# Three small edits where attention hands over to the experts: earlier weight requests, a shorter step list for one group, three subtractions on GpSimd

## The chip, the core and the metric

The kernel runs on one core of a Trainium2 chip. The metric is the device time of one execution in microseconds (us), the median over several runs. TensorE (PE) multiplies, with weight loads shown as an engine of their own (PEld); VectorE (DVE), ScalarE (ACT) and GpSimd (POOL) do the elementwise work; SyncE (SP) issues most of the DMAs, and GpSimd those that gather or scatter by index.

## The reference, cut to what matters

```python
a = softmax(phi)                                  # phi: 8 batches, 8 heads, 576 rows, 32 memories
k_m, v_m = a^T k, a^T v                           # 32 memory rows for each head
x = softmax(q k_m^T / 8) v_m                      # attention; rows become 4608 tokens of 512
e = argmax(x @ w_gate)                            # one of 8 experts for each token
gate = softmax(x @ w_gate)[e] * sigmoid(x @ w_output_gate)[e]
out[token] = gate * (relu(x @ w1[e]) @ w2[e])     # w1: 512x1024, w2: 1024x512
```

## The kernel before, in words

**Attention** is walked in 20 groups `g` (four pairs of batches, five groups each). A loop over `t` gives each group its steps in the order of a list of letters, `ORDER`, or an entry of `ORDERS` for some `t`: `S` scores turned and their maximum taken (`S0` is the transpose alone, `S1` the rest), `X` the exponential on ACT, `D` the division (a DVE sum, a POOL product), `B` a transpose back, `V0` the value product on PE and its copy `xo` on ACT, `V1` the store of `xo` to the DRAM table `xs`, `C` the scores of the next group, `M` and `m` memory work, `R` routing work. `LAG` says by how many `t` a step trails. `X1` and `D1` are the steps of one group earlier.

**The experts** work on slots of three (later two, one) blocks of 128 tokens. At group 17's `S0` the loop stops, and the first slot begins (`run`). From here attention goes on inside the slots: `hook` is called after each piece of PE work (in a three-block slot: 8 times in the first product, 12 times in the second) and takes three steps of the attention list and two of the routing. So an entry of the list decides at which piece of the expert's PE stream an attention step is put. A first-product piece is 12 matmuls `bps<-xh,whl` and `bps<-xl,whl` of 128x384, a second-product piece 6 matmuls `bps<-whl,hh` and `bps<-whl,hl` of 128x512.

**Weights** come in pieces `w` of 128x1024 (512 KB), eight for each slot, by SP's queue (`fetch`, L588). `split` makes two parts of a piece: ACT casts it to fp32r (`whl`, high, L599), and `flush` has DVE subtract that from `w` (`whl`, low, L613). PE multiplies in three passes: high by high, high by low, low by high. `parted` counts the pieces made; at the subtraction of the first slot's fourth, sixth and eighth piece it stands at 4, 6 and 8. Five buffers hold `w`, four hold `whl`.

**Routing.** When the last group of a batch pair has left, `rank` finds each token's expert and its place (`lm`, `w__2076`, `pm`, `ohg`, then a PE product `pr` with `strict`, L996, then `w__2076` again at L1006), writes the gates `gt` to columns of `xs` by four small DMAs on SP (L1025, L1028), and builds one-hot tables `Aw` on POOL (L1035). The gate stores of the second pair are held back until `run` begins. `route_early` and `table` then give the lists of token indices (`counts` is the PE product at L288, `bwb` feeds the one at L245). POOL gathers a slot's tokens `xg` by such a list (L550), the first slot's gates once more (`gidx`, L558), and scatters finished rows `y` (L1283). `y` has two buffers, so ACT's third `y` of a slot waits for the first scatter. The PSUM banks `ps` are three until the second slot has ended; `bpd` has two, shared by values, scores and the transposes `bpd<-ident,xg` (L1136) that turn the next slot's tokens.

```python
hh = relu(bank)              # ACT, L1314
hl = max(bank, 0) - hh       # DVE, L1315: after it the bank is free
```

Of the kernel before, what the change touches and what calls it, by code (L numbers as in the profile page):

```python
# [8 lines left out]
F32 = mybir.dt.float32  # L9
# [4 lines left out]
ALU = mybir.AluOpType  # L14
# [4 lines left out]
B, H, S, D, M = 8, 8, 576, 64, 32  # L19
# [19 lines left out]
ORDERS = {14: ["R0", "X", "S", "m", "V0", "M", "V1", "R1", "M", "m", "R2", "D", "B", "C"],  # L39
# [3 lines left out]
STEPS14 = {"R0": 12, "R1": 1, "R2": 8}  # L43
LAG = {"X": 1, "B": 2, "D": 1, "V": 3, "C": -1}
TICK = 0
# [30 lines left out]
def attention_moe(tc, phiT, kv, qT, wgo, wall, out):  # L76
    nc = tc.nc
    V, A, G, T = nc.vector, nc.scalar, nc.gpsimd, nc.tensor

    with contextlib.ExitStack() as ctx:  # L80
# [406 lines left out]
        def force():  # L487
            clock[0] += 1
            (rou if rou.gens else late if late.gens else att).step()
# [37 lines left out]
        m = NPE + NPT  # L527
# [27 lines left out]
        def gather_gates(z):  # L555
            V.tensor_scalar(gidx[:], z["idx"][0][:, 0:3], 2, None, ALU.logical_shift_left)
            for k in range(z["nb"]):
                G.indirect_dma_start(  # L558
                    out=z["xg"][:, k, 0:XQ], out_offset=None,
                    in_=xs[0:z["rows"]].rearrange("t (a q) -> (t a) q", a=4),  # L560
                    in_offset=bass.IndirectOffsetOnAxis(ap=gidx[:, k:k + 1], axis=0),
                    bounds_check=4 * z["rows"] - 1, oob_is_err=False)
# [5 lines left out]
        class Stream:  # L568
# [40 lines left out]
            def flush(self):  # L609

                if self.half:
                    w, hl = self.half
                    V.tensor_tensor(hl[:, 1], w[:], hl[:, 0].bitcast(F32), ALU.subtract)  # L613
                    self.half = None

            def take(self, i, u):
# [17 lines left out]
        def gathers(i, must=0):  # L634

            while gat[0] < min(gat[1], i + xgs.size):
                z = order[gat[0]]
                if not z["listed"]:
                    if gat[0] >= must:
                        break  # L640
                    force()
                    continue
                gather(z)
                gat[0] += 1
# [496 lines left out]
        def turn_first(z):  # L1141

            xg, n = z["xg"], z["nb"] * P
            xh, xl = z["x"] = mo.tile([P, 4, 3 * P], F32R, name="xh"), mo.tile([P, 4, 3 * P], F32R, name="xl")
            p0, p1, p2 = bank([512], "ps"), banks(), banks()
            pts = [p[:, 0:n] for p in (p0, p1[:, 0], p1[:, 1], p2[:, 0])]
            for c, pt in enumerate(pts):
                for k in range(z["nb"]):
                    T.transpose(pt[:, k * P:(k + 1) * P], xg[:, k, c * XQ:c * XQ + P], ident[:])
            for c, pt in enumerate(pts):  # L1150
                A.copy(xh[:, c, 0:n], pt)
                V.tensor_tensor(xl[:, c, 0:n], pt, xh[:, c, 0:n].bitcast(F32), ALU.subtract)  # L1152
# [255 lines left out]
        def settle():  # L1408

            att.finish()  # L1410
            pso.close()
            pa.close()
            env["hs"] = ctx.enter_context(tc.tile_pool(name="hs", bufs=1, side="right", reuse_waits="tile"))
            env["rl"] = ctx.enter_context(tc.tile_pool(name="rl", bufs=1, side="right", reuse_waits="tile"))
            env["xt"] = ctx.enter_context(tc.tile_pool(name="xt", bufs=2, side="right", reuse_waits="tile"))

            env["rep"] = env["rl"].tile([P, 4, P], BF16, name="rep")
            i4 = ident[:].rearrange("p (b i) -> p b i", b=4)
            for b in range(4):
                V.tensor_copy(env["rep"][:, b].rearrange("p (a i) -> p a i", a=4),  # L1420
                              i4[:, b:b + 1].to_broadcast([P, 4, 32]))
            grow(1)
            env["ps"] = ctx.enter_context(tc.tile_pool(name="p1", bufs=7, space=PSUM, reuse_waits="tile"))

        def run(st):

            lo, hi = st.lo, st.hi // 8
            while not order[lo]["known"]:
                force()
            while held:  # L1430
                held.pop(0)()
            st.fetch()
            if lo:
                gat[:] = lo, hi

            hooks = itertools.count()

            def hook():
                n = next(hooks)
                if lo == 0 and n == GATES[1]:  # L1440
                    gather_gates(order[0])
                if lo or n >= GATES[0]:
                    gathers(i)
                clock[0] += not att.gens
                att.step(HOOK[0])
                (rou if rou.gens else late).step(HOOK[1])

            for i in range(lo, hi):
                if i or lo:
                    gathers(i, i + 1)  # L1450
                if i == 0:
                    turn_first(order[0])
                    st.split(2)
                elif i == lo:
                    for c in range(5):
                        turn_x(order[i], c)

                def nxt(c):
                    if i + 1 < hi:
                        gathers(i, i + 2)  # L1460
                        turn_x(order[i + 1], c)

                if order[i]["nb"] > 1:
                    several(i, st, nxt, hook)
                else:
                    single(i, st, nxt)
                if "hs" not in env and (i == LAST or not att.gens):
                    settle()
# [5 lines left out]
        env["open"] = True  # L1474
        n = NPE + NPT + NPP
        run(stream)
        used = nc.values_load(slot[0:1, NSLOT:], min_val=0, max_val=NSS)  # L1477
        with tc.If(used > 0):
            run(Stream(n, n + 1))
            with tc.If(used > 1):  # L1480
                run(Stream(n + 1, n + 4))
                with tc.If(used > 4):
                    run(Stream(n + 4, NSLOT))
# [44 lines left out]
```

## Time and profile before

| what | value |
|---|---|
| median of 3 runs | 547.72 us (547.4 to 549.03) |
| the profiled execution's own time | 548.07 us |
| its span, first to last instruction | 546.3 us |
| PE busy | 507.7 us, 93% |
| DVE, ACT, POOL busy | 354.3, 286.6, 232.2 us |
| first expert matmul | 110.2 us |

The profiled execution lies 0.35 us above the median, and its span 1.77 us below its own time. The table is read thus: where PE is busy all the time, a change counts only if it takes away time in which PE waits, or adds some.

### The profile page before, as it was taken

Reading aid. Unit: us, or ns where it says so; the run is one execution under the profiler, and the core shown is the slowest. Engines: PE = TensorE matmul, PEld = TensorE weight load, DVE = VectorE, ACT = ScalarE, POOL = GpSimd, SP = SyncE. Lnnn points to the kernel's source line nnn. Section 1 sums busy time; section 2 is a strip of 40 time slices with the busy share of each in tenths; the row PEclk is TensorE's granted clock in tenths of the full one; section 3 lists DMA queues with packets and bytes.
Section 4 is the critical chain, followed back from the end, with each engine's and each line's share of the span. In section 5 each row is a group of like instructions: output and inputs, shape, how many; then the busy total and the mean of one; then the engine's idle time right before and its main releaser. Section 6 shows DMA issues by size and latency. Waiting matters only on the chain. (4 is left out here: it accounts for less than half of the span.)

```text
span 546.3 us, 10599 instructions
## 1 busy us (share of the span) xinstructions
PE 507.7 (93%) x3866; PEld 437.1 (80%) x3868; DVE 354.3 (65%) x798; ACT 286.6 (52%) x536; POOL 232.2 (43%) x239
## 2 busy tenths in 40 slices
PE   3788877999999999999999999999999999999993
PEld 2555555687789898897998989898999899898982
DVE  4275999869775569979446456953876297639310
ACT  3466775563444465353434546853776376548210
POOL 2242644616744052610278374565437453721101
PEclk9968998999999999999999999999999999999998
DMA  7999999997557758754465585865786577743001
GB/s 290 416 389 383 411 391 394 362 332 230 151 179 243 265 194 294 217 154 131 148 201 172 149 279 148 258 219 189 213 252 194 168 249 231 238 139 94 30 20 43
DMA packets 42093, 123.75 MB, mean 227 GB/s; under 512 B 10304, under 2 KB 10368, under 8 KB 41648
## 3 DMA queue, kind: packets, MB, share of 16 engines
q1 hardware_dynamic: 35136, 102.71, 56.7%
q0 software_dynamic: 6896, 20.28, 10.8%
q8 instruction: 32, 0.52, 0.4%
q14 instruction: 29, 0.24, 0.1%
HBM read 102.62 MB, written 20.35 MB: 225 GB/s over the span
## 5 line engine op out<-in xcount | busy, mean ns | idle before, releaser
L1347 PE MATMUL bps<-whl,hh 128*128 128x512 f32 x640 | 192.2, 393 | 0.0
L1310 PE MATMUL bps<-xh,whl 128*128 128x384 f32 x640 | 166.2, 336 | 0.7 <-DVE hl L1315 0.7
L613 DVE TENSOR_TENSOR whl<-w,whl 128x1024 fp32r<-128x1024 f32 x112 | 136.3, 1221 | 14.8 <-ACT whl L599 14.8
L1347 PEld LDWEIGHTS bps<-whl,hh 128*128 128x128 f32 x640 | 119.9, 188 | 24.4
L599 ACT CAST whl<-w 128x1024 fp32r<-128x1024 f32 x112 | 116.9, 1048 | 16.6 <-PE bps L1347 13.6
L1310 PEld LDWEIGHTS bps<-xh,whl 128*128 128x128 f32 x640 | 115.8, 188 | 2.3 <-DVE hl L1315 1.0
L544 POOL DMA_INDIRECT xg<-xs,idx_ql x84 | 100.4, 1195 | 25.7 <-issue 22.9
L1310 PE MATMUL bps<-xl,whl 128*128 128x384 f32 x320 | 107.1, 335 | 0.2 <-DVE xl L1152 0.2
L1347 PE MATMUL bps<-whl,hl 128*128 128x512 f32 x240 | 93.7, 390 | 0.0
L1315 DVE SCALAR_TENSOR_TENSOR hl<-bps,hh 128x384 fp32r<-128x384 f32 x80 | 43.7, 554 | 60.3 <-ACT hh L1314 60.3
L1314 ACT ACTIVATE hh<-bps 128x384 fp32r<-128x384 f32 x80 | 38.4, 494 | 64.6 <-PE bps L1310 64.5
L1283 POOL DMA_INDIRECT out<-y,idx_ol x23 | 25.4, 1106 | 102.9 <-ACT y L1282 54.3
L1310 PEld LDWEIGHTS bps<-xl,whl 128*128 128x128 f32 x320 | 60.1, 188 | 0.7 <-DVE xl L1152 0.4
L1347 PEld LDWEIGHTS bps<-whl,hl 128*128 128x128 f32 x240 | 45.1, 188 | 8.6
L903 POOL TENSOR_TENSOR ea<-ea,mx 128x512 f32<-128x512 f32 (+1 forms) x20 | 20.1, 1007 | 49.9 <-DVE mx L901 48.1
L1305 PE MATMUL bps<-xh,whl 128*128 128x384 f32 x128 | 37.7, 338 | 0.0
L1306 PE MATMUL bps<-xh,whl 128*128 128x256 f32 x128 | 35.7, 279 | 0.0
L1282 ACT ACTIVATE y<-bps,gx 128x512 f32<-128x512 f32 x19 | 13.1, 688 | 40.0 <-PE bps L1347 33.4
L1283 POOL DMA_INDIRECT out<-y,idx_ob x9 | 11.1, 1232 | 49.0 <-ACT y L1282 30.9
L936 PE MATMUL bpd<-ve_b,aT 64*128 64x144 f32 (+1 forms) x320 | 27.2, 319 | 2.7 <-DVE ea L893 1.4
L1282 ACT ACTIVATE y<-bps,xg 128x512 f32<-128x512 f32 x15 | 10.3, 689 | 34.7 <-DMA out<-y,idx_ob 15.0
L893 DVE STREAM_TRANSPOSE ea<-bpd 128x512 f32<-128x512 f32 (+1 forms) x20 | 13.2, 659 | 22.5 <-PE bpd L883 13.4
(283 smaller groups left out, 611.5 us busy)
## 6 DMA issues: line engine op xcount, KB each, us to landing
w<-wall SPq DMA_DIRECT2D x112, 512.0 KB, 4.7
kvt<-kv SPq DMA_DIRECT2D x32, 512.0 KB, 8.5
qt<-qT SPq DMA_DIRECT2D x16, 512.0 KB, 8.8
xs<-xo SPq DMA_DIRECT2D x12, 576.0 KB, 8.0
ph<-phiT SPq DMA_DIRECT2D x3, 1152.0 KB, 11.3
xs<-whl SPq DMA_DIRECT2D x4, 576.0 KB, 8.2
kv<-kv SPq DMA_DIRECT2D x4, 512.0 KB, 9.4
xg<-xs,idx_ql POOLq DMA_INDIRECT x84, 4.5
```

What stands on the lines that cost most here:

```text
L544: G.indirect_dma_start(out=z["xg"][:, k, XQ * b:XQ * b + XQ], out_offset=None, in_=xs[0:z["rows"]].rearrange("t (a q) -> (t a) q", a=4), i ...
L599: A.copy(hl[:, 0], w[:])
L613: V.tensor_tensor(hl[:, 1], w[:], hl[:, 0].bitcast(F32), ALU.subtract)
L936: T.matmul(px[to:to + n, r, sl], z["aT"][h, o:o + n], ves[2 * bp + b][h, g], start=True, stop=True)
L1282: A.activation(y[0:n], py[0:n], AF.Copy, scale=z["g"][0:n, k:k + 1] if z["quart"] else z["xg"][:, k, P:P + 1])
L1283: G.indirect_dma_start(out=out, out_offset=bass.IndirectOffsetOnAxis(ap=z["idx"][1][0:n, z["q0"] + k:z["q0"] + k + 1], axis=0), in_=y[0:n] ...
L1305: T.matmul(pb, w[:, 0, o:o + P], x[0][:, cc], start=(cc == 0), stop=False)
L1306: T.matmul(pb[:, 0:256], w[:, 1, o:o + P], x[0][:, cc, 0:256], start=False, stop=(cc == 3))
L1310: T.matmul(pb, w[:, b, o:o + P], x[a][:, cc, 0:n_], start=(n == 0), stop=(n == 11))
L1314: A.activation(h_[:, j], pb, AF.Relu)
L1315: V.scalar_tensor_tensor(l_[:, j], pb, 0.0, h_[:, j].bitcast(F32), ALU.max, ALU.subtract)
L1347: T.matmul(py[k], a, w[:, b, DM * f:DM * f + DM], start=(u == 4 and f == 0 and n == 0), stop=(u == 7 and f == 1 and n == len(ps) - 1))
```

## The change

It does three things. `run` asks for the weights that there is room for before it issues the held gate stores, not after. Group 17's list becomes shorter, 15 steps for 19, and is put in another order: three routing steps and two `m` go, one `M` comes, and `V0`, `V1` stand right behind `X1`. And the low part of three weight pieces is subtracted by GpSimd, not VectorE.

```diff
-          17: ["R4", "W", "S0", "S1", "X1", "X", "D1", "R0", "m", "D", "M", "B", "V0", "R1", "R1", "V1", "M", "m", "C"]}
+          17: ["R4", "W", "S0", "S1", "X1", "V0", "V1", "D1", "X", "D", "M", "M", "B", "M", "C"]}
...
                 if self.half:
                     w, hl = self.half
-                    V.tensor_tensor(hl[:, 1], w[:], hl[:, 0].bitcast(F32), ALU.subtract)
+                    e = G if self.parted in (4, 6, 8) else V
+                    e.tensor_tensor(hl[:, 1], w[:], hl[:, 0].bitcast(F32), ALU.subtract)
                     self.half = None
...
             while not order[lo]["known"]:
                 force()
+            st.fetch()
             while held:
                 held.pop(0)()
-            st.fetch()
```

What follows group 17 moves with it: its list ends four steps earlier, so the routing of the third batch pair and the groups 18 to 22 begin four steps earlier too, one hook and a third. Every line number behind the `flush` grows by one.

SP's queue where `run` begins, before (`gt` are the held gates, `w` the weight pieces four to seven):

```order
L700 DMA qt_1820<-qT 128x512
L1025 DMA xs_60<-gt_1408 128x4x16
L1028 DMA xs_60<-gt_1408 64x16
L1025 DMA xs_60<-gt_1408 128x4x16
L1028 DMA xs_60<-gt_1408 64x16
L588 ISA
L588 DMA w_1865<-wall 128x1024
L588 ISA
L588 DMA w_1867<-wall 128x1024
L588 ISA
L588 DMA w_1869<-wall 128x1024
```

The same place now:

```order
L701 DMA qt_1820<-qT 128x512
L588 ISA
L588 DMA w_1861<-wall 128x1024
L588 ISA
L588 DMA w_1863<-wall 128x1024
L588 ISA
L588 DMA w_1865<-wall 128x1024
L1026 DMA xs_60<-gt_1408 128x4x16
L1029 DMA xs_60<-gt_1408 64x16
L1026 DMA xs_60<-gt_1408 128x4x16
L1029 DMA xs_60<-gt_1408 64x16
```

Three weight requests passed the four gate stores.

GpSimd's queue from the divisions of group 15 and 16 on (`ea` products, the second slot's gather, `gidx`, the tables `Aw`, the first scatters), before:

```order
L916 TENSOR_TENSOR ea1_205<-ea1_205,sa_1989 128x16x32
L972 TENSOR_TENSOR w2__2077<-lg_1460,lm_2075 128x72
L903 TENSOR_TENSOR ea0_204<-ea0_204,mx_2109 128x16x32
L916 TENSOR_TENSOR ea2_206<-ea2_206,sa_2134 128x16x32
L558 DMA xg_1678<-xs_60,gidx_87 128x144 x3
L903 TENSOR_TENSOR ea1_205<-ea1_205,mx_2244 128x8x32
L916 TENSOR_TENSOR ea0_204<-ea0_204,sa_2258 128x16x32
L1035 TENSOR_SCALAR Aw_166<-iota_row_112,row_2085 128x128 x9
L1283 DMA out<-y_2371,idx_oa_80 4608x512
```

And now:

```order
L917 TENSOR_TENSOR ea1_205<-ea1_205,sa_2002 128x16x32
L973 TENSOR_TENSOR w2__2058<-lg_1460,lm_2056 128x72
L614 TENSOR_TENSOR whl_2086<-w_1865,whl_2086 128x1024
L904 TENSOR_TENSOR ea0_204<-ea0_204,mx_2092 128x16x32
L917 TENSOR_TENSOR ea2_206<-ea2_206,sa_2114 128x16x32
L558 DMA xg_1678<-xs_60,gidx_87 128x144 x3
L904 TENSOR_TENSOR ea1_205<-ea1_205,mx_2233 128x8x32
L614 TENSOR_TENSOR whl_2241<-w_1952,whl_2241 128x1024
L917 TENSOR_TENSOR ea0_204<-ea0_204,sa_2252 128x16x32
L1036 TENSOR_SCALAR Aw_166<-iota_row_112,row_2066 128x128 x9
L917 TENSOR_TENSOR ea1_205<-ea1_205,sa_2361 128x8x32
L1284 DMA out<-y_2388,idx_oa_80 4608x512
```

The sixth weight's subtraction stands ahead of `gidx`, the eighth's between `gidx` and the tables `Aw`, and one more product ahead of the first scatter; the fourth's stands further up, ahead of group 15's division.

PE in the first slot's second product, around the values of group 16 (`bpd<-ve_b,aT`) and a transpose of the next slot's tokens (`bpd<-ident,xg`), before:

```order
L1347 MATMUL bps<-whl,hl 128x512
L1347 MATMUL bps<-whl,hh 128x512
L936 MATMUL bpd<-ve_b,aT 128x144 x8
L1347 MATMUL bps<-whl,hh 128x512
L1347 MATMUL bps<-whl,hl 128x512
L1347 MATMUL bps<-whl,hh 128x512 x2
L1347 MATMUL bps<-whl,hl 128x512
L1347 MATMUL bps<-whl,hh 128x512
L1136 MATMUL bpd<-ident,xg 128x128 x3
```

And now:

```order
L1348 MATMUL bps<-whl,hl 128x512
L1348 MATMUL bps<-whl,hh 128x512
L937 MATMUL bpd<-ve_b,aT 128x144 x8
L1137 MATMUL bpd<-ident,xg 128x128 x3
L1348 MATMUL bps<-whl,hh 128x512
L1348 MATMUL bps<-whl,hl 128x512
```

The six matmuls between the values and the transposes are gone from there; the same holds for group 17's values and the last transposes, nearer the slot's end.

## Rows read from the trace of the kernel before

**Rows 1.** The profile's page, part 1: busy time of each engine, share, instructions.

```profile
PE 507.7 (93%) x3866; PEld 437.1 (80%) x3868; DVE 354.3 (65%) x798; ACT 286.6 (52%) x536; POOL 232.2 (43%) x239
```

**Rows 2.** Stretches of the span: length, then each engine's busy us (instructions), PE clock.

```profile
110.00:170.00 60.00, 57.15 (x419) 49.32 (x420) 46.22 (x112) 29.88 (x51) 27.49 (x28) 1.00 0.71 226
170.00:250.00 80.00, 80.00 (x438) 71.92 (x438) 59.36 (x157) 41.25 (x62) 26.83 (x25) 1.00 0.69 219
260.00:532.00 272.00, 272.00 (x1428) 248.59 (x1427) 160.98 (x267) 147.60 (x273) 130.52 (x111) 1.00 0.58 180
```

**Rows 3.** PE's timeline: start, us, instruction [idle before, what ended it].

```profile
122.97 0.44 PE L1310 MATMUL bps<-xh,whl 128*128 128x384 f32 x1 [0.66 <-DVE hl L1315]
...
135.27 0.19 PE L996 MATMUL pr<-ohg,strict 128*128 128x72 bf16 x1 [0.80 <-DVE ohg L978]
...
141.32 0.18 PE L288 MATMUL pr<-ohc,ones_b 128*128 128x8 bf16 x1 [0.54 <-DVE w__2076 L1006]
...
161.92 0.83 PE L245 MATMUL pr<-bwb,Aw 128*128 128x18 bf16 x27 [0.71 <-DVE bwb L234]
...
253.70 0.54 PE L245 MATMUL pr<-bwl,Aw 128*128 128x90 bf16 x9 [0.31 <-DVE bwl L234]
```

**Rows 4.** SP's queue, in order of time.

```profile
110.56 0.77 SPq L1025 DMA_DIRECT2D xs<-gt  x1
...
114.55 11.83 SPq L588 DMA_DIRECT2D w<-wall  x7
```

**Rows 5.** ACT's timeline.

```profile
119.30 1.05 ACT L599 CAST whl<-w 128x1024 fp32r<-128x1024 f32 x1 [2.64 <-DMA w<-wall]
...
156.35 0.69 ACT L1282 ACTIVATE y<-bps,xg 128x512 f32<-128x512 f32 x1 [3.39 <-DMA out<-y,idx_oa]
156.94 1.18 ACT L938 COPY xo<-bpd 128x576 f32<-128x576 f32 x2
157.99 1.07 ACT L599 CAST whl<-w 128x1024 fp32r<-128x1024 f32 x1
```

**Rows 6.** DVE's timeline.

```profile
128.55 1.59 DVE L971 TENSOR_TENSOR w__2076<-lg,lm 128x72 f32<-128x72 f32 x1
...
135.05 0.17 DVE L978 TENSOR_TENSOR ohg<-desc,pm 128x72 bf16<-128x72 f32 x1
...
141.05 0.22 DVE L1006 TENSOR_TENSOR w__2076<-ohg,pr 128x72 f32<-128x72 bf16 x1
...
159.09 1.23 DVE L613 TENSOR_TENSOR whl<-w,whl 128x1024 fp32r<-128x1024 f32 x1 [3.72 <-ACT whl L599]
160.23 0.55 DVE L1315 SCALAR_TENSOR_TENSOR hl<-bps,hh 128x384 fp32r<-128x384 f32 x1
```

**Rows 7.** GpSimd's timeline.

```profile
99.11 0.62 POOL L903 TENSOR_TENSOR ea<-ea,mx 128x256 f32<-128x256 f32 x1 [4.86 <-DVE mx L901]
...
107.71 1.90 POOL L903 TENSOR_TENSOR ea<-ea,mx 128x512 f32<-128x512 f32 x1 [0.35 <-DVE mx L901]
115.08 1.05 POOL L903 TENSOR_TENSOR ea<-ea,mx 128x512 f32<-128x512 f32 x1 [5.48 <-DVE mx L901]
...
128.97 1.07 POOL L916 TENSOR_TENSOR ea<-ea,sa 128x512 f32<-128x512 f32 x1
...
139.25 1.72 POOL L558 DMA_INDIRECT xg<-xs,gidx  x1 [2.92 <-DVE gidx L556]
...
145.20 7.46 POOL L1035 TENSOR_SCALAR Aw<-iota_row,row 128x128 bf16<-128x128 bf16 x9
152.84 1.10 POOL L1283 DMA_INDIRECT out<-y,idx_oa  x1 [0.17 <-issue]
```

**Rows 8.** PE's waits on ACT's copy of the values, earlier in attention.

```profile
80.33 0.67 PE L883 MATMUL bpd<-qt,kT 64*32 64x256 f32 x16 [0.25 <-ACT xo L938]
...
95.33 0.76 PE L936 MATMUL bpd<-ve_b,aT 64*128 64x144 f32 x8 [0.78 <-ACT xo L938]
```

**Rows 9.** DVE's timeline, a subtraction at the handover.

```profile
107.48 1.22 DVE L613 TENSOR_TENSOR whl<-w,whl 128x1024 fp32r<-128x1024 f32 x1
```

## The prediction

> **What bounds the kernel now.** The page's first part comes first: PE is busy 93% of the span, the next engine 65% [rows 1]. A share says nothing of a stage, so the stretches come next. Once the experts run, PE is busy for all of 170 to 250 us and all of 260 to 532; between 110 and 170, where attention is finished inside the first two slots, it is busy 57.15 of 60 us [rows 2]. The clock column reads 1.00 (the upper level, 2.4 GHz) in all three stretches, so no clock is to be won there. What can be won by a change at the handover is therefore PE's idle time behind 110 us, and PE's timeline names it: 0.66 us for `hl` at 122.97, 0.80 for `ohg` at 135.27, 0.54 for the second `w__2076` at 141.32, 0.71 for `bwb` at 161.92, and 0.31 for `bwl` at 253.70 [rows 3]. That is 3.02 us, 0.55% of 548.07. Every one of them is a wait for DVE. 0.3%, about what a measurement of this kernel can tell from no change, is 1.6 us. So the change must close more than half of those gaps and open few.
>
> **The weight requests.** The four gate stores keep SP from 110.56 until the first weight request at 114.55 [rows 4]. ACT sits 2.64 us until 119.30 for that piece, the fourth, and only then casts it [rows 5]; the two `hh` behind the cast are late, so is `hl`, and PE waits 0.66 us for the bank. Now the request goes out at about 110.5, four us earlier. If it lands four us earlier as well, at 115.3, it is there before ACT comes to it (ACT stands before the cast from 119.30 - 2.64 = 116.66 on). Two loads of `q` are still on their way; even 2 us lost to them would leave ACT without a wait. The gap goes: **-0.66**. Bounds: 0, if the piece lands no sooner, and -0.66. The gate stores come three requests later, some 3 us, and end at about 117.4; the gather that reads their columns stands on GpSimd behind the fourth weight's subtraction and a product, at about 122, so nothing is added there. The weight requests behind them are needed several us later.
>
> **The subtractions.** On DVE each takes 1.22 us [rows 9]. GpSimd's price for this form is in no row. Its products of two SBUF tensors take 0.62 us for 256 columns and 1.05 for 512 [rows 7]; the difference carried on gives 1.05 + 2 x 0.43 = 1.9 us for 1024, and I take 2.0 us. The other end is the 7.46 us for nine `Aw` of 128 columns [rows 7], 0.83 us each: eight of these, 6.6 us, if GpSimd is as slow with the fp32r output as with that bf16 form. The nearest row is the float32 product, whose shape and operands are those of the subtraction, so 2.0 us. (The Trainium skill, "GPSIMD Engine Reference", section 3.1, has 4497 ns for such an add over 2048 elements; half of that, 2.25 us, is an estimate from that page and would move the sum by under 0.1 us. No run here shows it.)
>
> The sums are not independent, though. The product at 107.71 took 1.90 us where its like take 1.05, and it started while DVE's subtraction at 107.48 ran; DVE's little `w__2076` at 128.55 took 1.59 us, and it ended just as GpSimd's product at 128.97 did (128.97 + 1.07 = 130.04) [rows 6, 7, 9]. I read this as the two engines keeping each other out while both read two SBUF tensors. So a subtraction on GpSimd can hold DVE's next two-tensor instruction for up to 2.0 us. (The Trainium skill says so too, "SBUF — State Buffer", section "Who interferes with whom": a VectorE instruction with two SBUF inputs and a GpSimd one that reads SBUF exclude each other for the whole instruction. It speaks against this change, and the rows agree. By it the next term is -0.2; without it, -0.8.)
>
> **The wait for `ohg`.** PE came to `strict` at 135.27 - 0.80 = 134.47. Now it comes earlier: by the 0.66 us above, and by one piece of six matmuls, since a value step and one piece stand ahead of it where a value step and two stood; a piece is about 1.5 us. So at 132.3. DVE's side: the list ends four steps earlier, and I lay DVE's instructions end to end from the first of `rank`, at about 124.5: maximum 0.2, `w__2076` 0.8, an `hl` not before its `hh` at 126.0, 0.5; group 18's transpose and maximum 1.4. That is 127.9. The next is a two-tensor product, and GpSimd has just begun the sixth weight (127.7 to 129.7, behind the second slot's gather and a product). So it runs at 129.8; then 0.2, 0.2, an `hl` 0.5, a sum and a reciprocal 0.9, a transpose 0.7: 132.3. Here GpSimd's product of those sums is in the way until 132.8. `ohg` is there at 133.0, against 135.22 before [rows 6], and PE waits 0.6 us: **-0.2**. Bounds: -0.8 if nothing collides, +0.5 if one more GpSimd instruction of 1.05 us gets in ahead.
>
> **The wait for the second `w__2076`.** PE comes to `counts` 3 pieces, the scores and a transpose after `strict`, now at about 138.5. DVE has until then: `ohg` 133.0, two small ones 0.9, an `hl` 0.5, the seventh weight 1.2, three small ones 0.3, `xl` not before 136.3, 0.5, `gidx` 0.1, transpose, maximum and sum of group 19 1.2: 138.2. The eighth weight, 1.2 us, stood in this row before and is on GpSimd now. **-0.54**; bounds -0.54 and 0.
>
> **The wait for `bwb`.** It was DVE standing 3.72 us at 159.09 for a cast that came at 157.99, behind the third `y` at 156.35, which itself waited 3.39 us for the first scatter, issued at 152.84 [rows 5 to 7]. `bwb` stood behind that subtraction on DVE. Now DVE has `bwb` ahead of it, and ACT's two `xo` copies (1.18 us) stand ahead of the third `y`. **-0.71**, if the chain through GpSimd does not become later: `gidx` at 137.2 for 139.25; to the start of `Aw` the 5.95 us of before and the eighth weight's 2.0; `Aw` 7.46, a product 0.62. The first scatter goes at 153.5 for 152.84, so the third `y` at 157.1, the cast at 157.8, its subtraction until 160.1, `hl` until 160.6. PE needs that bank for the second slot's fourth piece, at about 161.1; the end of `hl` before was 160.78 [rows 6]. So it holds, with half a us to spare. Bounds -0.71 and 0.
>
> **The wait for `bwl`** belongs to the last batch pair's routing, which starts four steps earlier against the same stream of weights: **-0.3**; bounds -0.31 and +0.3.
>
> **What the reordering adds.** Twice a transpose of the next slot's tokens now stands right behind a pair of value products. Those take both `bpd` buffers, so the transpose must wait until ACT has copied the first. One copy is 0.59 us (half of 1.18 [rows 5]) and can start when the first value product is done, half-way through the pair; PE then waits some 0.35 us, and some 0.45 the second time, where ACT has the first `y` in front. Waits of this kind earlier in attention were 0.25 and 0.78 us [rows 8], which bounds the two by 0.5 and 1.6: **+0.8**. The other steps that moved cost PE the same at their new places.
>
> **The sum**: -0.66 - 0.2 - 0.54 - 0.71 - 0.3 + 0.8 = -1.6 us. The profiled execution would go from 548.07 to 546.5 and its span to 544.7; the median shown is 0.35 us lower, so I predict 546.1. The likeliest case alone runs from 545.4 to 546.8.
>
> **The rivals.** *All gaps close.* If GpSimd's subtractions fall into moments when DVE reads one tensor or PSUM, `ohg` is in time and the new waits are 0.5 us together: -0.66 - 0.80 - 0.54 - 0.71 - 0.31 + 0.5 = -2.5, 545.2. For it speaks that DVE is busy only 46.22 of the 60 us [rows 2]; against it that it is busy without a break where `rank` runs.
>
> *The saving is given back at once.* DVE loses to the lock what it is relieved of: the wait for `ohg` stays at 0.8, that for `counts` at 0.5, and only the weight request, `bwb` and `bwl` count against the new waits at their upper bound: -0.66 - 0.71 - 0.3 + 1.6 = -0.1; with the `q` loads ahead of the weight in the queue, so that the first edit does not do what it says, +0.6. So 547.6 to 548.3. The two long rows, 1.90 and 1.59 us, speak for it.
>
> *GpSimd becomes the chain, and the kernel slower.* The eighth weight lies on GpSimd's way to `Aw` and the first scatter. At a price p the second slot's fourth piece starts at 160.6 + (p - 2.0) at the earliest; before it started at 162.6. From p = 4.0 on nothing is gained, from 5.6 on the loss is over 1.6 us, and at 6.6 us it is 2.6: 550.3. For it speaks only the `Aw` row; against it the float32 products.
>
> **Chances.** All gaps close 0.2; the forecast 0.45, of which 0.3 over and 0.15 under 1.6 us; given back 0.2; GpSimd's chain, or another new wait of its size, 0.15. So faster by over 0.3% 0.5, within 0.3% 0.35, slower 0.15. The range takes in the first three cases and the spread of the runs shown (0.3%): 544.5 to 548.6, with the slower case left out.
>
> **What would show it.** In the changed profile ACT has no wait for `w` near 119, and PE none for `hl` near 122; `strict` waits for `ohg` some 0.6 us near 133, `counts` and `bwb` not at all; PE waits for ACT's `xo` at two transposes; three GpSimd subtractions take 1.9 to 2.2 us, longer where they start within one of DVE's; the first scatter goes near 153.5. The prediction is wrong if a subtraction on GpSimd takes over 4 us, if the weight still lands near 119, or if PE shows a wait over 1 us at a place not named here.

## The result, and the profile after

The changed kernel takes 550.4 us (median of 22 executions, 548.74 to 557.81), the kernel before, run beside it, 547.33 (22 executions, 545.78 to 551.15): ratio 1.0058 [1.0042, 1.0074]. It is slower by some 3 us, where 1.6 us less were predicted. In two of the five sets of experiments below (the first and the fourth) the kernel before itself took 556.6 and 560.3 us, matmuls late in the stream waited for nothing that the trace shows, and some executions were slow as a whole (the ratios leave those out, the medians do not), so the kernels of those two sets are compared with each other alone.

The profiled execution after took 550.03 us, span 548.2, which is 1.96 us more than the one before. Page, part 1 (busy time of each engine), of the changed kernel, beside [rows 1]:

```profile
PE 506.4 (92%) x3868; PEld 435.9 (80%) x3868; DVE 355.8 (65%) x795; ACT 287.4 (52%) x536; POOL 231.0 (42%) x242
```

The stretches of [rows 2], after (length, busy us of PE, PEld, DVE, ACT, POOL, PE clock, DMA share, GB/s):

```profile
110.00:170.00 60.00, 56.25 (x416) 48.01 (x414) 47.10 (x109) 30.51 (x51) 32.24 (x31) 1.00 0.70 220
170.00:250.00 80.00, 80.00 (x441) 72.18 (x440) 62.82 (x163) 40.81 (x61) 25.81 (x25) 1.00 0.71 225
260.00:532.00 272.00, 272.00 (x1427) 248.63 (x1426) 162.83 (x268) 148.87 (x274) 125.71 (x111) 1.00 0.59 181
```

As before, nothing is lost behind 170 us. In the first stretch PE is busy 0.9 us less, and GpSimd 4.75 us more. PE's timeline after, the rows that wait (in brackets the idle time and what ended it), against [rows 3]:

```profile
135.31 0.19 PE L997 MATMUL pr<-ohg,strict 128*128 128x72 bf16 x1 [2.22 <-DVE ohg L979]
...
143.79 0.55 PE L1137 MATMUL bpd<-ident,xg 128*128 128x128 f32 x3 [0.25 <-ACT xo L939]
...
153.03 0.55 PE L1137 MATMUL bpd<-ident,xg 128*128 128x128 f32 x3 [0.29 <-ACT xo L939]
...
161.74 0.45 PE L1311 MATMUL bps<-xh,whl 128*128 128x384 f32 x1 [0.55 <-ACT y L1283]
...
164.41 0.45 PE L1311 MATMUL bps<-xh,whl 128*128 128x384 f32 x1 [0.29 <-DVE hl L1316]
```

The waits of [rows 3] for `hl`, the second `w__2076`, `bwb` and `bwl` are gone, 2.22 us of them. In their place stand 0.54 us for `xo`, 0.84 for the scatter's chain (`y`, `hl`), and the wait for `ohg` is 2.22 us where it was 0.80. What held `ohg` stands on DVE's timeline:

```profile
125.50 0.23 DVE L972 TENSOR_TENSOR w__2057<-lg,lm 128x72 f32<-128x72 f32 x1
...
128.55 3.87 DVE L975 TENSOR_TENSOR w__2057<-w__2057,desc 128x72 f32<-128x72 f32 x1
132.45 0.23 DVE L977 TENSOR_REDUCE pm<-w__2057 128x9 f32<-128x72 f32 x1
...
134.53 0.72 DVE L979 TENSOR_TENSOR ohg<-desc,pm 128x72 bf16<-128x72 f32 x1
```

A product of 72 columns, 0.2 us of work, lasted 3.87 us. GpSimd's timeline over the same time and behind it:

```profile
119.52 2.48 POOL L614 TENSOR_TENSOR whl<-w,whl 128x1024 fp32r<-128x1024 f32 x1 [2.39 <-ACT whl L599]
...
127.64 1.07 POOL L917 TENSOR_TENSOR ea<-ea,sa 128x512 f32<-128x512 f32 x1
128.65 0.32 POOL L973 TENSOR_TENSOR w__2058<-lg,lm 128x72 f32<-128x72 f32 x1
128.93 2.39 POOL L614 TENSOR_TENSOR whl<-w,whl 128x1024 fp32r<-128x1024 f32 x1
131.26 1.06 POOL L904 TENSOR_TENSOR ea<-ea,mx 128x512 f32<-128x512 f32 x1
...
139.53 1.04 POOL L558 DMA_INDIRECT xg<-xs,gidx  x1 [4.36 <-DVE gidx L556]
...
143.78 2.40 POOL L614 TENSOR_TENSOR whl<-w,whl 128x1024 fp32r<-128x1024 f32 x1
...
147.17 7.33 POOL L1036 TENSOR_SCALAR Aw<-iota_row,row 128x128 bf16<-128x128 bf16 x9
...
155.25 1.10 POOL L1284 DMA_INDIRECT out<-y,idx_oa  x1 [0.17 <-issue]
```

The three L614 rows are the subtractions, 2.39 to 2.48 us each. The product was issued at 128.55, in the last 0.2 us of L917, and ended at 132.42, just behind the end of L904 at 132.32: it stood through everything that GpSimd had ready, one instruction after the other. From there all is later than forecast: `gidx` 139.53 for 137.2, the first scatter 155.25 for 153.5 [before in rows 7: 139.25 and 152.84]. ACT's third `y` waits for that scatter, and a store of `xo` goes out on SP's queue just ahead of it (ACT, then SP):

```profile
117.45 1.99 ACT L599 CAST whl<-w 128x1024 fp32r<-128x1024 f32 x2
...
161.00 0.69 ACT L1283 ACTIVATE y<-bps,xg 128x512 f32<-128x512 f32 x1 [5.31 <-DMA out<-y,idx_oa]
161.59 1.04 ACT L599 CAST whl<-w 128x1024 fp32r<-128x1024 f32 x1
...
154.53 0.38 SPq L1062 DMA_DIRECT2D xs<-xo  x1
```

### The profile page after: what moved, and what is told of

The parts are those of the page before. It is cut to its first block, busy times and chain, and to the rows that moved or that the text cites. A ratio compares the mean times of both kernels' runs of the same rounds, so it can differ in the third digit from the quotient of the medians.

```text
span 548.2 us, 10598 instructions
## 1 busy us (share of the span) xinstructions
PE 506.4 (92%) x3868; PEld 435.9 (80%) x3868; DVE 355.8 (65%) x795; ACT 287.4 (52%) x536; POOL 231.0 (42%) x242
## 5 line engine op out<-in xcount | busy, mean ns | idle before, releaser
L614 DVE TENSOR_TENSOR whl<-w,whl 128x1024 fp32r<-128x1024 f32 x109 | 133.1, 1225 | 10.7 <-ACT whl L599 10.7
L544 POOL DMA_INDIRECT xg<-xs,idx_ql x84 | 96.4, 1147 | 25.9 <-issue 24.1
L904 POOL TENSOR_TENSOR ea<-ea,mx 128x512 f32<-128x512 f32 (+1 forms) x20 | 20.1, 1006 | 50.5 <-DVE mx L902 50.4
L937 PE MATMUL bpd<-ve_b,aT 64*128 64x144 f32 (+1 forms) x320 | 25.9, 311 | 2.7 <-DVE ea L894 1.4
L1129 DVE TENSOR_TENSOR xh<-xt,xh 128x192 fp32r<-128x192 f32 x16 | 5.6, 352 | 33.3 <-ACT xh L1128 33.3
```

Of the source, the lines that this page charges most:

```text
L544: G.indirect_dma_start(out=z["xg"][:, k, XQ * b:XQ * b + XQ], out_offset=None, in_=xs[0:z["rows"]].rearrange("t (a q) -> (t a) q", a=4), i ...
L614: e.tensor_tensor(hl[:, 1], w[:], hl[:, 0].bitcast(F32), ALU.subtract)
L904: G.tensor_tensor(eav, eav, mx[:, 0:n].unsqueeze(2).to_broadcast([P, n, M]), ALU.subtract)
L937: T.matmul(px[to:to + n, r, sl], z["aT"][h, o:o + n], ves[2 * bp + b][h, g], start=True, stop=True)
```

## The experiments

All kernels are the changed kernel with one or two of its parts taken back, or one thing moved or cut in two. "Wait" is PE's idle time at `strict`, "product" the duration of the 72-column product on DVE, "clock" the lowest granted clock in stretches of 2 us between 130 and 148 us, all from the one profiled execution. The ratio is to the kernel before on the same chip. For the first and the fourth set see the first section.

| set and kernel | on GpSimd | wait | product | clock | median us | ratio [interval] |
|---|---|---|---|---|---|---|
| the change | 4, 6, 8 | 2.22 | 3.87 | 1.00 | 550.4 | 1.0058 [1.0042, 1.0074] |
| 1 none | - | 0.38 | 0.23 | 1.00 | 549.98 | 0.9844 [0.9792, 0.9896] |
| 1 list only | - | 1.41 | 0.22 | 1.00 | 551.44 | 0.9869 [0.9814, 0.9924] |
| 1 subtractions only | 4, 6, 8 | 1.35 | 2.31 | 1.00 | 558.03 | 1.0001 [0.9962, 1.004] |
| 1 request only | - | 0.79 | 0.22 | 1.00 | 558.58 | 1.0003 [0.994, 1.0067] |
| 2 the change | 4, 6, 8 | 2.73 | 4.37 | 1.00 | 550.68 | 1.0054 [1.0025, 1.0082] |
| 2 sixth on DVE | 4, 8 | 2.09 | 2.06 | 0.50 | 548.76 | 1.0026 [1.0007, 1.0045] |
| 2 none | - | 0.59 | 0.22 | 1.00 | 546.03 | 0.998 [0.996, 1.0] |
| 2 sixth in halves | 4, 6, 8 | 2.97 | 4.62 | 0.54 | 550.98 | 1.0066 [1.0041, 1.0091] |
| 3 fourth | 4 | 0.26 | 0.22 | 1.00 | 546.51 | 0.9988 [0.996, 1.0016] |
| 3 sixth | 6 | 1.56 | 3.21 | 1.00 | 547.17 | 1.0002 [0.9978, 1.0025] |
| 3 eighth | 8 | 1.08 | 0.22 | 1.00 | 548.12 | 1.0013 [0.9987, 1.0038] |
| 3 none | - | 1.41 | 0.22 | 1.00 | 547.19 | 0.9991 [0.9968, 1.0013] |
| 4 product moved | 4, 6, 8 | 0.87 | moved | 1.00 | 553.48 | 0.9888 [0.9845, 0.9931] |
| 4 none, product moved | - | 0.82 | moved | 1.00 | 553.19 | 0.9896 [0.9829, 0.9962] |
| 4 the change | 4, 6, 8 | 2.23 | 3.87 | 0.50 | 554.67 | 0.995 [0.9907, 0.9992] |
| 4 none | - | 1.27 | 0.23 | 1.00 | 552.53 | 0.9867 [0.9801, 0.9932] |
| 5 product moved | 4, 6, 8 | 0.91 | moved | 1.00 | 547.82 | 1.0016 [0.999, 1.0042] |
| 5 the change | 4, 6, 8 | 2.43 | 4.08 | 0.50 | 549.74 | 1.0044 [1.0028, 1.006] |

### Set 1: the three parts apart

None on GpSimd (new list, new request):

```
-                    e = G if self.parted in (4, 6, 8) else V
-                    e.tensor_tensor(hl[:, 1], w[:], hl[:, 0].bitcast(F32), ALU.subtract)
+                    V.tensor_tensor(hl[:, 1], w[:], hl[:, 0].bitcast(F32), ALU.subtract)
```

> The weight requests and the new list of group 17, with all subtractions on VectorE. Theory A (the loss comes from the subtractions on GpSimd, which hold back VectorE's product ahead of ohg and the first scatter): the wait of strict falls from 2.2 us to under 1.0, the second slot has no wait for y, and the kernel is 1 to 2.5 us faster than before, ratio 0.9955 to 0.998. Theory B (the loss comes from the new list: transposes behind the values, DVE work in another order): the kernel stays slower than before by 2 us or more, ratio over 1.0035. Theory C (the gate stores pushed back by the requests hurt): the same as B here.

Subtractions only (old list, `st.fetch()` behind the held stores again):

```
-          17: ["R4", "W", "S0", "S1", "X1", "V0", "V1", "D1", "X", "D", "M", "M", "B", "M", "C"]}
+          17: ["R4", "W", "S0", "S1", "X1", "X", "D1", "R0", "m", "D", "M", "B", "V0", "R1", "R1", "V1", "M", "m", "C"]}
...
-            st.fetch()
             while held:
                 held.pop(0)()
+            st.fetch()
```

> Only the three subtractions go to GpSimd; list and requests are those of before. Theory A: slower than before by 1 to 4 us, ratio 1.002 to 1.007, with a long wait of PE for ohg or for the second slot's banks. Theories B and C: within 0.2% of before, ratio 0.998 to 1.002.

List only (subtractions on DVE and the request behind the stores):

> Only group 17's list is new. Theory A: PE gains the waits for counts and bwb (1.2 us) and pays two waits for ACT's copy (0.5 us); the wait for the fourth weight stays: ratio 0.998 to 1.001. Theory B: slower by 2 us or more, ratio over 1.0035.

Request only (old list, subtractions on DVE):

> Only the weight requests go ahead of the held gate stores. Theory A: ACT has no wait for the fourth weight, PE none for hl near 122, 0.66 us won at most: ratio 0.998 to 1.0005. Theory C: slower by over 1 us, ratio over 1.002, with the second slot's gather waiting for the gate stores.

The two kernels with the new list ran some 7 us below the two with the old one, so the list is not the loss; how much of those 7 us is the list's and how much the waits that nothing explains can't be told from this set. The subtractions alone were expected at a ratio of 1.002 to 1.007 and came out at 1.0001 [0.9962, 1.004]: this set does not show their loss in time, only the waits in their profile, 1.35 us for `ohg` and 2.11 for `bwb` [0.71 before in rows 3]. The set shows one more thing. With the early request alone, SP asks for the fourth weight as part of the x3 at 111.52, ahead of the stores, and yet the cast waits for it as long as before, and PE for `hl` (SP, ACT and PE of that kernel):

```profile
111.52 1.98 SPq L588 DMA_DIRECT2D w<-wall  x3
...
120.48 1.05 ACT L599 CAST whl<-w 128x1024 fp32r<-128x1024 f32 x1 [2.54 <-DMA w<-wall]
...
124.15 0.44 PE L1310 MATMUL bps<-xh,whl 128*128 128x384 f32 x1 [0.56 <-DVE hl L1315]
```

The stretches of that kernel fit (length, PE busy, clock, DMA share, GB/s): the DMA engines are full.

```profile
108.00:112.00 4.00, 3.57 (x59) 1.00 1.01 392
112.00:116.00 4.00, 3.85 (x22) 1.00 1.02 380
116.00:120.00 4.00, 4.00 (x25) 1.00 1.03 372
```

With the list alone the cast still waits 1.28 us for the weight, but PE does not wait for `hl`. With the subtractions alone, so with the old list and the old request, the cast waited 1.48 us and PE did not wait for `hl` either; with list and request together the cast waits between nothing and 1.53 us from one profile to the next. So PE waits for `hl` only in the two profiles in which the cast waited over 2.5 us, and what of that is the list's and what the request's is not shown.

### Set 2: which subtraction, and how the product is held

The whole change again:

> The change as it is, again, so that it stands beside its parts on one chip. Theory A (the loss comes from the subtractions on GpSimd): the wait for the first one-hot again above 1.5 us, the product of 72 columns on VectorE held for over 3 us, and a time 3 to 5 us above that of the variant with no subtraction on GpSimd. Rival B (the parts do not differ, and what separated them was when they ran): the two times within 1.5 us.

The sixth on DVE: `if self.parted in (4, 8)`.

> GpSimd subtracts the fourth and the eighth weight, VectorE the sixth. Theory A: the wait for the first one-hot falls from 2.2 us to between 0.4 and 1.4 us, the product of 72 columns takes 0.23 us again, the time lies 1 to 2 us below the whole change, and still 1 to 3 us above the variant with none on GpSimd, because the eighth subtraction still delays the gate's results and the first scatter. Rival A2 (only the sixth costs anything): the time is that of the variant with none. Rival B: all within 1.5 us.

None on GpSimd again:

> The new request and the new list, with all subtractions on VectorE. Theory A: the fastest of the four, 3 to 5 us below the whole change, waits of the matmuls behind 110 us about 1.1 us in sum. Rival B: within 1.5 us of the whole change.

The sixth in halves:

```
-                    e.tensor_tensor(hl[:, 1], w[:], hl[:, 0].bitcast(F32), ALU.subtract)
+                    for c in ([slice(0, 512), slice(512, 1024)] if self.parted == 6 else [slice(0, 1024)]):
+                        e.tensor_tensor(hl[:, 1, c], w[:, c], hl[:, 0, c].bitcast(F32), ALU.subtract)
```

> The whole change, with the sixth weight's subtraction on GpSimd cut into two instructions of 512 columns. If VectorE's waiting product loses to every instruction that GpSimd has ready (theory A1), cutting changes nothing: the product is held for 3.5 to 4.2 us and the wait for the one-hot stays above 2 us. If the pair goes to the one that waits as soon as GpSimd's running instruction ends (theory A3), the product is held for at most 1.6 us and the wait falls below 1 us, the time by 1 to 1.5 us.

Theory A holds: none is the fastest, 4.65 us below the whole change (547.52 is the median of before in this set), and the kernel without the sixth lies between. Theory A1 holds too. In the kernel with halves, DVE and GpSimd:

```profile
127.89 4.62 DVE L976 TENSOR_TENSOR w__2057<-w__2057,desc 128x72 f32<-128x72 f32 x1
...
127.62 1.06 POOL L918 TENSOR_TENSOR ea<-ea,sa 128x512 f32<-128x512 f32 x1
128.63 0.31 POOL L974 TENSOR_TENSOR w__2058<-lg,lm 128x72 f32<-128x72 f32 x1
128.90 2.51 POOL L615 TENSOR_TENSOR whl<-w,whl 128x512 fp32r<-128x512 f32 x2
131.37 1.04 POOL L905 TENSOR_TENSOR ea<-ea,mx 128x512 f32<-128x512 f32 x1
```

The product stood from the last 0.8 us of L918 through four further GpSimd instructions, and the seam between the two halves did not let it in. What I had expected of the kernel without the sixth was half wrong: its wait stayed at 2.09 us and the product at 2.06, because GpSimd was late, and the product ran into L917, L973 and L904 in a row.

### Set 3: each subtraction alone

`if self.parted in (4,)`, `(6,)` and `(8,)`, and none beside them.

> GpSimd subtracts the fourth weight alone. Theory C (the fourth is what makes the first one-hot late: it puts GpSimd's gathers and its products back by some 3 us, so that VectorE's product of 72 columns meets a GpSimd queue that never stands): the wait for the one-hot is 1.5 to 2.5 us, the product is held for about 2 us, and the time lies 1.5 to 3 us above the variant with none. Rival D (the sixth does it, as it lies right beside the product): the wait is 0.4 to 0.8 us and the time that of the variant with none within 0.7 us.

> GpSimd subtracts the sixth weight alone. Theory C: GpSimd is not late when the sixth comes, so the product is held for one subtraction at most, 1 to 2.4 us, the wait for the one-hot is 0.8 to 2 us, and the time lies 0.5 to 2 us above the variant with none. Rival D: wait above 2 us, time 2 to 4 us above.

> GpSimd subtracts the eighth weight alone. It comes behind the first one-hot, so no theory expects a longer wait there. Theory C: GpSimd's rows and the first scatter come 1.3 to 2.4 us later than with none, still before the store that frees the output's buffer is needed; PE waits at most 0.5 us for it; the time is within 0.7 us of the variant with none. Rival E (the first scatter sets the end of the group): 1 to 2 us above it.

> The new request and the new list, all subtractions on VectorE, beside the three. Theories C, D and E alike: the lowest time or level with the eighth alone, 1 to 2 us below the kernel before, waits of the matmuls about 1.1 us in sum.

Theory C wanted 1.5 to 3 us from the fourth alone, theory D 2 to 4 from the sixth alone, and neither came. The fourth costs nothing that the times show, and in this profile PE waits 0.26 us. One profile does not settle theory C, though: up to the eighth subtraction, behind 140 us, this kernel and that of set 2 without the sixth are the same instructions, and there the product was held for 2.06 us and PE for 2.09 (set 2, then this kernel; DVE and GpSimd of each):

```profile
129.18 2.06 DVE L975 TENSOR_TENSOR w__2057<-w__2057,desc 128x72 f32<-128x72 f32 x1
...
128.82 1.06 POOL L917 TENSOR_TENSOR ea<-ea,sa 128x512 f32<-128x512 f32 x1
...
130.75 0.22 DVE L975 TENSOR_TENSOR w__2057<-w__2057,desc 128x72 f32<-128x72 f32 x1
...
129.18 1.21 POOL L917 TENSOR_TENSOR ea<-ea,sa 128x512 f32<-128x512 f32 x1
```

From the first expert matmul (110.25 and 111.80 us) DVE came to the product after 18.9 us in both, and GpSimd to L917 after 18.6 us there and 17.4 here: by 1.2 us of GpSimd's the product meets a whole row or none. The sixth alone holds the product for 3.21 us and `strict` for 1.56. The eighth alone makes the scatter's chain late, which PE's timeline of that kernel shows:

```profile
164.18 0.44 PE L1311 MATMUL bps<-xh,whl 128*128 128x384 f32 x1 [0.96 <-ACT y L1283]
```

By the middles of the ratios, against 0.9991 for none in this set, the three singles add up to -0.2 + 0.6 + 1.2 = 1.6 us; the three together cost some 3 to 4 us against none (1.0058, 1.0054 and 1.0044 against 0.998 and 0.9991; only 1.0054 and 0.998 are of one set). Each interval is 1.2 to 1.5 us to either side, so that by them no single one is clear of none, and the parts may simply add up; that they enhance one another is not shown.

The kernel with none shows that the new list alone can meet the same hold, from the other side. Here the sixth subtraction is DVE's own, and ran into GpSimd (DVE, then GpSimd):

```profile
127.47 2.35 DVE L613 TENSOR_TENSOR whl<-w,whl 128x1024 fp32r<-128x1024 f32 x1
...
127.67 1.06 POOL L916 TENSOR_TENSOR ea<-ea,sa 128x512 f32<-128x512 f32 x1
128.67 1.31 POOL L972 TENSOR_TENSOR w__2058<-lg,lm 128x72 f32<-128x72 f32 x1
```

DVE stood until L916 had ended, 1.1 us, and then it did get in: GpSimd's L972, 0.3 us of work, stood 1 us for it. So theory A1 holds for the product and not for every DVE instruction. With such holds the wait with none is 0.38, 0.59, 1.27 or 1.41 us from one execution to the next.

### Sets 4 and 5: the held product taken off DVE

```
+            if bp == 2:
+                G.tensor_tensor(w1_[:], w1_[:], dscb, ALU.mult)
             yield
-            V.tensor_tensor(w1_[:], w1_[:], dscb, ALU.mult)
+            if bp != 2:
+                V.tensor_tensor(w1_[:], w1_[:], dscb, ALU.mult)
             yield
```

> The whole change, with the third gate's product of 72 columns moved from VectorE to GpSimd, right behind GpSimd's difference of 72 columns and ahead of the sixth subtraction, so that nothing on VectorE waits for the pair between the two maxima. Theory F (the product held on VectorE makes the one-hot late): the wait for the one-hot falls from 2.2 to 2.7 us to under 0.9 us, and the time by 1.5 to 3 us below the whole change. Rival G (the one-hot is late because GpSimd or the reductions are, whoever makes the product): the wait stays above 1.5 us, the time within 0.8 us.

> The same move with all subtractions on VectorE. Theory F: the wait for the one-hot is 0.2 to 0.8 us, as often or lower than with none (0.38, 0.59 and 1.41 in three profiles), the time within 0.7 us of that variant or up to 1 us below it. Rival G: the same wait as with none.

> The whole change beside the moved product. Both theories: a wait of 2 to 3 us for the one-hot, 3 to 4.7 us above the variant with none.

> None on GpSimd beside the moved product. Both theories: 0.5 to 1.5 us below the kernel before.

The wait fell from 2.23 to 0.87 us, as theory F has it; the times of this set spread over 10 us and settle nothing. So the pair ran again:

> The whole change with the third gate's product on GpSimd, again, since the first call's times spread too far to tell 2 us. Theory F: a wait for the one-hot of 0.5 to 1.2 us, and 1 to 2.5 us below the whole change. Rival G: within 0.7 us of it.

> The whole change beside it. Both theories: a wait of 2 to 3 us for the one-hot, and 2.5 to 3.5 us above the kernel before.

In set 5 the moved product saves 549.74 - 547.82 = 1.92 us by the medians, as theory F has it; the intervals of the two ratios just overlap. PE, DVE and GpSimd of that kernel:

```profile
133.00 0.19 PE L1000 MATMUL pr<-ohg,strict 128*128 128x72 bf16 x1 [0.91 <-DVE ohg L982]
...
130.62 2.33 DVE L982 TENSOR_TENSOR ohg<-desc,pm 128x72 bf16<-128x72 f32 x1
...
128.17 0.33 POOL L975 TENSOR_TENSOR w__2057<-w__2057,desc 128x72 f32<-128x72 f32 x1
128.47 2.38 POOL L614 TENSOR_TENSOR whl<-w,whl 128x1024 fp32r<-128x1024 f32 x1
```

GpSimd makes the product in 0.33 us ahead of its subtraction, DVE has the maximum at 128.53 instead of 131.37 in the whole change of this set, and only `ohg` itself, two SBUF tensors again, is held (2.33 us for 0.17). The held product is therefore what made the wait long, by 1.5 us. Moving it does not bring back all of the loss: 1.0016 is still above none on GpSimd (0.998 and 0.9991), and the waits for `y` and `hl` stay. The whole change beside it shows what the wait costs besides: its stretches (length, PE busy, clock, DMA share, GB/s) round the wait of 2.43 us that ends at 134.22, and PE's rows:

```profile
130.00:132.00 2.00, 1.79 (x10) 1.00 0.40 91
132.00:134.00 2.00, 0.00 (x0) 1.00 0.50 199
134.00:136.00 2.00, 1.77 (x14) 0.67 0.02 4
136.00:138.00 2.00, 2.00 (x36) 0.50 0.39 51
138.00:140.00 2.00, 2.00 (x11) 0.97 0.82 276
...
134.22 0.19 PE L997 MATMUL pr<-ohg,strict 128*128 128x72 bf16 x1 [2.43 <-DVE ohg L979]
...
144.14 0.55 PE L1137 MATMUL bpd<-ident,xg 128*128 128x128 f32 x3 [0.25 <-ACT xo L939]
```

PE stood still for a whole stretch, and the granted clock then fell to 0.50, the lower level (1.2 GHz), before it came back. Against the upper level that is 2 x (0.33 + 0.50 + 0.03) = 1.7 us of clock, an estimate. PE's rows give it directly: from `strict` to the transposes that wait for `xo` it took 144.14 - 134.22 = 9.92 us, where the first profile of the change, at the upper level all the way, took 143.79 - 135.31 = 8.48. That is 1.4 us, and the other three profiles in which the clock fell have 9.94 to 9.98.

The version that the experiments point to is the new list and request with all subtractions on DVE. It is faster than the change in both sets that hold the two (2 and 4), clearly in set 2. Against the kernel before, 0.998 [0.996, 1.0] and 0.9991 [0.9968, 1.0013] do not show a gain for sure.

## Why the prediction was wrong

**The step that failed is the wait for `ohg`.** The prediction had DVE's product stand behind one subtraction ("So it runs at 129.8"), with a wait of 0.6 us (-0.2), and for a bound "+0.5 if one more GpSimd instruction of 1.05 us gets in ahead". Measured: 2.22 us, +1.42. Three things add up. The sixth subtraction began at 128.93 instead of 127.7, half a us of it because the whole handover was later; it took 2.39 us instead of 2.0; and DVE did not get its turn at the end, but stood through L904 too: 1.2 + 0.4 + 1.0 = 2.6 us, about the 2.4 by which the product ended late (132.42 for 130.0). PE itself came to `strict` at 133.09 for 132.3, so 0.6 + 2.4 - 0.8 = 2.2. The rule that I weighed was right in kind. The Trainium skill ("SBUF — State Buffer", "Summary: rules for kernel authors") has the engine that issues second stand until the first is done; the trace agrees that it stands, but here it went on standing through three or four further GpSimd instructions that began after it (products of 3.87, 4.37 and 4.62 us). By that the term is not -0.2 but +1.4, beyond the bound of +0.5 and beyond the rival "given back at once", which had this wait stay at 0.8. The kernel before showed the like once, and the prediction read past it: `w__2076`, issued at 128.55, ended behind GpSimd's product that began only at 128.97 [rows 6, 7]. In front of that product GpSimd had a gather under way until 128.95:

```profile
127.19 1.76 POOL L550 DMA_INDIRECT xg<-xs,idx_ga  x1 [0.30 <-issue]
```


**The scatter's chain** is the second miss; the prediction gave its condition, "if the chain through GpSimd does not become later". The third `y` came at 161.00 instead of 157.1. Of these 3.9 us, `gidx` gives 2.3 (139.53 for 137.2, as it follows `ohg` on DVE), the way from `gidx` to the first scatter takes 0.6 off (155.25 - 139.53 = 15.7 for 16.3, the eighth subtraction's 2.4 us included), and the way from the scatter to `y` gives 2.2: 161.00 - 155.25 = 5.75 us where [rows 5, 7] had 156.35 - 152.84 = 3.5. This last size I had carried over unasked, and the list is what changed it: it puts `V1`, the store of `xo`, further ahead, and this store now goes out just before the scatter (154.53 us, above) where it went out 7.9 us behind it (160.74). In the 15 profiles in which SP issues the store 0.3 to 0.7 us ahead of the scatter, the third `y` comes 5.1 to 5.75 us behind the scatter; in the other two with the new list, without the sixth in set 2 and the whole change in set 4, the store goes 1.76 us behind the scatter and `y` comes after 3.1; with the old list it is 3.1 to 4.2. That the store's transfer delays the scatter's is argued from this order, not shown by an experiment. The whole change of set 4 has no wait for `y` or `hl`, though its eighth subtraction too is GpSimd's. `bwb` is on time as forecast (-0.71), but 0.84 us for `y` and `hl` take its place. The rival "GpSimd becomes the chain" named this place, with a price of 6.6 us for a subtraction; the place was right, the price was 2.4, and by its own sum nothing is lost below 4. That its 550.3 us lies beside the measured 550.4 is chance. In set 5, with the product moved, `gidx` goes at 137.23 and PE still waits 0.39 + 0.29 us here.

**What held, or only in size.** Gone, as forecast: `hl` at the fourth weight (-0.66), `counts` (-0.54), `bwl` (-0.31). Whether the first of these went the way that I gave is not shown: with the request alone the wait for the weight stays, and with the list alone `hl` is in time too. The two new waits behind value products are 0.25 + 0.29 = 0.54 us for 0.8. A subtraction on GpSimd takes 2.39 to 2.48 us for 2.0. (The estimate of 2.25 us from the Trainium skill, "GPSIMD Engine Reference", section 3.1, was nearer than mine. Worked through the prediction's own chain it starts the product 0.25 us later, so it would have moved the sum by about that, not "by under 0.1 us".)

**The sum, measured**: -0.66 - 0.54 - 0.71 - 0.31 + 1.42 + 0.54 + 0.84 = +0.6 us where -1.6 was forecast. From the start of the first expert matmul to the end of PE's last, the profiled execution after takes 427.92 us for 426.91, +1.0; 0.4 of that stands in none of the waits named. The rest of the 1.96 us between the two profiled executions lies outside: +0.5 before the handover, where this first matmul starts anywhere from 109.5 to 114.4 us in the profiles shown whatever the kernel, and +0.4 behind the last matmul, which stays open.

**The medians differ by 3.07 us, 1.1 more than the profiles.** Each profile is one execution, and the two lie 0.7 us above and 0.4 below the medians, well inside the spread. Part of the 1.1 may be the clock, which the prediction had put at "no clock is to be won"; it did not ask what could be lost. Of the six profiles with a wait over 2 us at `strict` four show the clock fall behind it; of the other 14 (waits up to 1.56 us) none does. The two profiles of the change that do not show it are those of the first section and of set 2. How often it falls in the timed executions is not shown: in set 2 the whole change has a mean granted clock of 0.977 and none 0.980, but in set 4 none has the lower one (0.976 for 0.978), and in set 5 the change and the moved product have 0.977 both.

## What to carry to other kernels

When work is moved to GpSimd, look at what GpSimd has ready behind it, not at its duration alone: DVE's small product on two SBUF tensors waited for the end of the whole row, and if a chain that PE waits for goes through it, a few tenths of relief become two us. Order such small products ahead of the long instruction, or on GpSimd itself in front of it, which here took the wait from 2.4 to 0.9 us. A long wait of PE can be dearer than its length: behind four of the six over 2 us the clock fell, for 1.4 us more. And a request issued earlier need not land sooner where the DMA engines are full, while a store moved ahead can land in front of a transfer that something waits for.

## What was not expected of the hardware

- DVE's product of 72 columns was held for 2.06 to 4.62 us through one to four GpSimd instructions that began after it, one behind the other, and cutting one of them in two did not let it in. DVE's subtraction of 1024 columns did get in between two (set 3), and GpSimd's 0.3 us difference then took 1.31 us. What decides who goes first at such a seam is open.
- After PE stood still for 2.09, 2.23, 2.43 and 2.97 us the granted clock fell to 0.50 to 0.54 for some 4 us; after 2.22 and 2.73 us it did not.
- In the one profile with the request alone, a weight asked for ahead of the stores made ACT wait about as long as before (2.54 us for 2.64): DMA share 1.01 to 1.03 from 108 to 120 us.
- The first scatter let `y` go after 5.1 to 5.75 us where a store of `xo` was issued 0.3 to 0.7 us ahead of it, and after 3.1 where the same store was issued 1.76 us behind it.
- PE waited behind 270 us for nothing that the trace shows: 7.6 and 6.9 us in the two kernels of set 1 with the old list (executions of 562 and 563 us), none in the two with the new one, 2.5 to 2.8 in all four of set 4. Why is open.
